# Attention with a following prelu layer on one core: when a group's half sums are swapped and added, and when its turned tiles are made, on VectorE

## The chip, the cores and the metric

The kernel runs on one core of a Trainium2 chip. The metric is device microseconds of one execution; the kernel before takes 435.62 us (median of 3 runs, 435.51 to 436.47).

## The reference, cut to what matters

```
q, k, v: (8 batches, 12 heads, 448 rows, 64)   g_q, g_k: (64,)
q_n = q / sqrt(mean(q*q, -1) + 1e-6) * g_q          # k_n likewise, with g_k
attn = softmax(q_n @ k_n^T / 8);   x = attn @ v      # heads side by side: (3584, 768)
h = x @ w_in                                         # (3584, 2048)
g = max(h, 0) + alpha * min(h, 0)
out = g @ w_out                                      # (3584, 768)
```

## The kernel before, in words

**Groups.** The 96 pairs of batch and head are taken four at a time: 24 groups `y`, three to a batch. The 448 rows of a head are 64 x 7, so a group has seven tiles of scores (y, 0) to (y, 6).

**Preparing a group** takes a chain over four engines. SyncE's queue loads q and k (`load_qk`). GpSimd squares them (L193). VectorE sums the squares: `reduce` (L214), one for q and one for k. From group 9 on the data lies so that a reduce gives half sums only: each partition has the sum over one half of the 64 columns. `fold` swaps the halves between blocks of 32 partitions (four short reductions, L231) and adds them (L234). ScalarE takes the root (`root`, L244 and L245, an Ln and an Exp), GpSimd scales q and k by it (`scale`, L251), VectorE transposes blocks of 32 x 32 (`flip`, L359, once for q and once for k), and ScalarE multiplies the turned k by the product of the two gains (`weigh`, L369). `turn` (L371) makes those flips of a group that are still missing.

**Bursts.** The instruction order is written out by a planner in bursts 0 to 68, each engine running its own list in order. In a burst TensorE makes two to four tiles of scores (L415) in the PSUM tiles `sc`, of which there are two, and ScalarE makes their exponentials (`soft`, L429). In some bursts TensorE also adds up the denominators (`dn` or `dnb`, L440 and L464, with ScalarE's `log` and `invert` behind them) and the product with v (`av`, `avb`, L440), which VectorE divides into `xT` (`muls`, L539).

**Units** fill the rest of a burst (`gaps[n]`, by a table at L998). `up(b, ft)` is one of 16 blocks of x @ w_in: six matmuls (L554), then alpha times it on ScalarE (L594), then the max on VectorE (L598), which frees the PSUM tile. `down` is one tile of g @ w_out; `quad_a`, `quad_b` and `quad_c` together make two tiles by the seven products of Strassen's scheme (L681), and VectorE adds each product up (L700, L705, L710, L722, L727, L729, L739, L744). Its operand sums are made by `mix_two` (L669, L670) and `mix_rest` (L677).

**PSUM tiles.** `hT`, `qx`, `qz`, `qc` and `dnb` take turns in two tiles; a name with an `a` behind it (`hTa`, `qza`, `qca`), `dn` and `av` share one more, "the wide one". A matmul into a tile waits until its last reader is through.

**Jobs.** What VectorE does to prepare groups is put behind units as jobs (`jobs[n]`). A `quad` takes one job behind a product and all that are left behind its last one, as here:

```
def quad_b(tile, spare, jobs=()):        # L715
    ...
    nc.vector.tensor_add(out=w, in0=p[:, :OH], in1=u2)            # L722
    some(jobs)                                                    # one job
    ...
    nc.vector.tensor_add(out=o, in0=z[:, :OH], in1=w)             # L727
    send(tile + 1, 1, o)
    nc.vector.tensor_add(out=u2, in0=z[:, :OH], in1=u2)           # L729
    while jobs:
        some(jobs)                                                # the rest
```

`quad_a` takes one job behind L700, one behind L705 and the rest behind L710; `quad_c` one behind L739 and the rest behind L744; a `down` takes all at its end, sums ahead of its copy (L627) and flips behind it. Behind an `up`, one job is taken, and from burst 20 on only after the first, third and fifth of a burst; what is left is done at the burst's end. The root of group y stands in burst `root_at[y]`, the reduces of most groups one burst earlier.

Of the kernel before, what the change touches and what calls it, by code (L numbers as in the profile page):

```python
# [21 lines left out]
def kernel(  # L22
# [27 lines left out]
    TD = min(3 * G, NG)  # L50
# [320 lines left out]
    def turn(y):  # L371

        if y >= TD:
            for nm in "qk":
                if (y, nm) not in qkT:
                    flip(y, nm)
            return
        if y <= G or y > 2 * G:
            ps = [psf.tile([128, 512], FP32, name="tps", tag="mm") for _ in "qk"]
        else:  # L380
            ps2 = psa.tile([128, 2, 512], FP32, name="tps2", tag="acc")
            ps = [ps2[:, 0], ps2[:, 1]]
        tps = [
            t[:, : S].bitcast(FP16).rearrange("p (j c) -> p j c", j=J) for t in ps
        ]
        for tp, nm in zip(tps, "qk"):
            for j in range(J):
                nc.tensor.transpose(
                    tp[:, j, :], qs[y, nm][:, j].rearrange("p h d -> p (h d)"), ident
                )  # L390
        for tp, nm in zip(tps, "qk"):
            t = att.tile([128, J, 2, 64], FP16, name=f"{nm}T", tag=f"{nm}T", bufs=2)
            o = t.rearrange("p j g c -> p j (g c)")
            if nm == "q":
                nc.vector.tensor_copy(out=o, in_=tp)
            else:
                nc.vector.tensor_scalar(
                    out=o, in0=tp, scalar1=gain[:, 0:1], scalar2=None, op0=ALU.mult
                )
            qkT[y, nm] = t  # L400
# [4 lines left out]
    def pre(ys):  # L405
        return len(ys) == 1 and ys[0] >= PRE and ys[0] % G == G - 1
# [205 lines left out]
    def down(tile, oh, jobs=(), spare=False):  # L612

        op = bank("op", spare)
        for ft in range(NF):
            nc.tensor.matmul(  # L616
                out=op[:, :OH],
                lhsT=gT[:, ft, ts(tile % J, 128)],
                rhs=w_out_sb[:, ft, ts(oh, OH)],
                start=(ft == 0),  # L620
                stop=(ft == NF - 1),
            )
        for f, a in jobs:
            if f not in (turn, flip, weigh):
                f(*a)
        o = result()
        nc.vector.tensor_copy(out=o, in_=op[:, :OH])  # L627
        for f, a in jobs:
            if f in (turn, flip, weigh):
                f(*a)  # L630
        send(tile, oh, o)
# [203 lines left out]
    while m < NG * J or steps:  # L835
        n = len(bursts)
# [20 lines left out]
        while len(bursts[n]) < limit and m < NG * J:  # L857
            y, j = divmod(m, J)
# [13 lines left out]
    def at(n, f, *a):  # L872
        prep.setdefault(max(int(n), 0), []).append((f, a))

    def after(n, f, *a):
        post.setdefault(max(int(n), 0), []).append((f, a))
# [7 lines left out]
        (y, den_at[y - 2] - pre((y - 2,))) for y in range(TD, NG) if y % G == 1  # L884
    )
    turns = {n: y for y, n in turn_at.items()}
    jobs, root_at, nexts = {}, {}, {}
    for y in range(G, NG):

        early = y < G + 2  # L890
        if early:
            n = turn_at[y - 1] + 1
        elif y == G + 2:
            n = den_at[G - 1]
        elif y == 2 * G:
            n = turn_at[y] - 4
        elif y % G == 1:
            n = den_at[y - 4] - 1 - pre((y - 2,))
        elif y % G:
            n = den_at[y - G] - pre((y - G,))  # L900
        else:
            n = av_at[y - 4]
        low = y > 3 * G + 1
        if low:
            nexts[root_at[y - 2]] = y
        elif y in (3 * G - 1, 3 * G):

            after(den_at[G] - (y < 3 * G), load_qk, y)
        else:
            at(n - (6 if early or y % G == G - 1 and pre((y - G,)) else 3 if y == 2 * G else 4 if y < 3 * G else 5), load_qk, y)  # L910
        root_at[y] = n + 1 + (y in (G + 2, 3 * G))
        third = y % G == G - 1 and pre((y - G,))
        for nm in "qk":
            if y != 2 * G:
                after(n - 2 - third + (low and y % G == 1) - (low and third and y != 20), square, y, nm)
            if early:
                after(n, reduce, y, nm, (0, 1) if (y, nm) == (G, "k") else None)
            else:
                now = jobs.setdefault(n + (y == G + 2 and nm == "k") - (low and third), [])
                now.append((reduce, (y, nm)))  # L920
                if nm == "k" and y > TD:
                    now.append((fold, (y,)))
        if y == 3 * G:
            after(n, *jobs[n].pop()[:1], y, "k")
        roots[root_at[y]] = y
    at(av_at[G] - 6, load_v, 1)
    for b in range(2, B):
        after(av_at[G * b - 1] + 1, load_v, b)
# [28 lines left out]
    gaps = [[] for _ in range(NB)]  # L957
# [148 lines left out]
    for n in range(NB):  # L1106
# [70 lines left out]
        if n in roots:  # L1177
            y = roots[n]
# [42 lines left out]
        ups_first = gaps[n] and gaps[n][0][0] is up  # L1221
# [7 lines left out]
        if flips:  # L1229
            jobs.setdefault(n, []).extend(flips)  # L1230
        turned = n in turns and gaps[n] 
        if turned and not ups_first and turns[n] >= TD:
            jobs.setdefault(n, []).extend([(turn, (turns[n],)), (weigh, (turns[n],))])
        elif turned and turns[n] >= TD:
            y = turns[n]
            todo = [(flip, (y, nm)) for nm in "qk" if (y, nm) not in qkT] + [(weigh, (y,))]
            jobs[n] = todo + jobs.get(n, [])
        elif turned and turns[n] != 2 * G + 1:
            turn(turns[n])
        for k, (f, a) in enumerate(gaps[n]):  # L1240
            if k == 1 and turned and turns[n] == 2 * G + 1:
                turn(turns[n])
            spare = k in spare_at or f is up and a in forced
            if f is down:
                down(*a, jobs.pop(n, ()), spare)
            elif f is not up:
                f(*a, jobs.pop(n, []))
            else:
                f(*a, spare)
                done += 1  # L1250
                if n in jobs and not (lead and done < 5) and (
                    n < av_at[2 * G - 1] or done % 2
                ):
                    g, c = jobs[n].pop(0)
                    g(*c)
                    if not jobs[n]:
                        del jobs[n]
                while late and done == late[0][0]:
                    _, g, c = late.pop(0)
                    g(*c)  # L1260
# [50 lines left out]
```

## Time and profile before

| | us |
|---|---|
| median of 3 runs | 435.62 |
| the profiled execution | 432.87 |
| its span, first to last instruction | 431.1 |
| TensorE busy (matmuls) | 404.6 |
| VectorE busy | 281.3 |
| ScalarE busy | 270.5 |
| GpSimd busy | 268.0 |

The profile is of one execution. Busy times are sums over an engine, so they do not tell which engine sets the time in which stretch. A row of the timeline has the start, the duration, the engine, the line, the operation, what it writes and reads, and how many were merged; in brackets stands how long the engine was idle just before and whose work ended that. The view of waits adds these up by pairs: total, times, longest. The view of windows gives, for a stretch, each engine's busy time and the clock granted to TensorE.

### The profile page before, as it was taken

What the parts mean: (1) busy time and instruction counts of PE and PEld (TensorE: products, weight loads), DVE (VectorE), ACT (ScalarE), POOL (GpSimd) and SP (SyncE); (2) the same over time, 40 slices, a digit from 0 to 9 for tenths busy, and PEclk for the clock granted to TensorE, in tenths of its full rate; (3) what the DMA queues carried; (4) which work ended last, traced back from release to release, by engine and by line L of the source; (5) the groups of instructions that cost most, each with busy time, mean ns of one, the idle gap of its engine ahead of it and who ended that gap; (6) DMA issues with size and microseconds to landing.
All of it is one profiled execution on the core that took longest, in us unless ns stands there. A gap on an engine that the chain in (4) does not pass through costs nothing.

```text
span 431.1 us, 11989 instructions
## 1 busy us (share of the span) xinstructions
PE 404.6 (94%) x5083; PEld 210.0 (49%) x5083; DVE 281.3 (65%) x495; ACT 270.5 (63%) x405; POOL 268.0 (62%) x184
## 2 busy tenths in 40 slices
PE   7789999999998989999999979899998999999996
PEld 3344454544545435544455435445454445655564
DVE  3876874576458576886879673977667745465322
ACT  5887777656845876467777785586576786125210
POOL 5699993698667969196571839367840715600780
PEclk9999999999999999999999998999999999999999
DMA  8899999957381996349581795449602600320133
GB/s 266 227 210 208 173 193 235 250 153 141 90 205 40 246 183 156 85 100 234 119 202 40 185 232 124 96 102 231 136 21 58 100 2 22 75 56 0 26 95 101
DMA packets 37221, 58.39 MB, mean 135 GB/s; under 512 B 4768, under 2 KB 28976, under 8 KB 37168
## 3 DMA queue, kind: packets, MB, share of 16 engines
q1 hardware_dynamic: 23232, 45.43, 41.8%
q0 software_dynamic: 13536, 11.81, 18.3%
q8 instruction: 39, 0.64, 0.6%
q10 hardware_dynamic: 400, 0.39, 0.3%
q14 instruction: 14, 0.11, 0.1%
HBM read 58.40 MB, written 11.01 MB: 161 GB/s over the span
## 4 chain that ended last, share of the span: by engine, by line
PE 53%; DVE 15%; DMA 11%; ACT 8%; POOL 7%; issue 3%; SPq 1%; DVEq 0%; POOLq 0%
PE hT L554 16%; PE hTa L554 6%; PE qx L681 5%; PE sc L415 4%; ACT expT L429 4%; PE oq L681 3%; DVE sp L214 3%; DMA nat<-in_k_dram 3%; DMA nat<-in_q_dram 3%; PE op L616 2%; PE qc L681 2%; DVE gT L598 2%; DMA arena<-in_k_dram 2%; PE qz L681 2%; PE oqm L681 2%
## 5 line engine op out<-in xcount | busy, mean ns | idle before, releaser
L429 ACT ACTIVATE expT<-sc 128x896 f16<-128x896 f32 x168 | 147.4, 912 | 43.9 <-PE sc L415 43.7
L554 PE MATMUL hT<-xT,w_in_sb 128*128 128x448 f16 x558 | 116.7, 353 | 4.5 <-DVE gT L598 4.0
L554 PEld LDWEIGHTS <-w_in_sb 128*128 128x128 f16 x768 | 73.0, 98 | 79.6 <-issue 15.4
L251 POOL TENSOR_TENSOR qs<-nat,rr 128x896 f16<-128x896 f32 x30 | 63.9, 2230 | 36.4 <-ACT rr L245 27.2
L594 ACT ACTIVATE gT<-hT,cols 128x448 f16<-128x448 f32 x92 | 58.1, 633 | 42.0 <-PE hT L554 42.0
L598 DVE TENSOR_TENSOR gT<-hT,gT 128x448 f16<-128x448 f32 x93 | 57.6, 620 | 39.9 <-ACT gT L594 39.6
L193 POOL TENSOR_TENSOR nat<-nat 128x896 f32<-128x896 f32 x30 | 50.6, 1691 | 37.9 <-DMA nat<-in_k_dram 22.1
L415 PE MATMUL sc<-qT,kT 64*32 64x448 f16 (+1 forms) x1092 | 53.8, 358 | 7.1 <-ACT expT L429 4.2
L681 PEld LDWEIGHTS <-gT 128*128 128x128 f16 x352 | 33.5, 98 | 25.1 <-issue 4.1
L554 PE MATMUL hTa<-xT,w_in_sb 128*128 128x448 f16 x198 | 42.8, 352 | 0.0
L539 DVE TENSOR_TENSOR xT<-av,rden 64x448 f16<-64x448 f32 (+1 forms) x37 | 27.2, 735 | 17.1 <-ACT expT L429 5.9
L415 PEld LDWEIGHTS <-kT 64*32 64x32 f16 (+1 forms) x1092 | 15.8, 93 | 40.5 <-issue 35.3
L214 DVE TENSOR_REDUCE sp<-nat 128x28 f32<-128x896 f32 x30 | 31.9, 1076 | 0.0
L594 ACT ACTIVATE gT<-hTa,cols 128x448 f16<-128x448 f32 x33 | 21.0, 636 | 16.3 <-PE hTa L554 16.3
L598 DVE TENSOR_TENSOR gT<-hTa,gT 128x448 f16<-128x448 f32 x33 | 20.4, 617 | 15.3 <-ACT gT L594 15.3
L616 PE MATMUL op<-w_out_sb,gT 128*128 128x384 f16 x160 | 27.4, 326 | 0.0
L440 PEld LDWEIGHTS <-vt 64*32 64x32 f16 x1344 | 19.8, 92 | 14.7 <-issue 5.4
L440 PE MATMUL av<-expT,vt 64*32 64x448 f16 x896 | 24.3, 350 | 2.4 <-DVE osb L729 1.3
L669 POOL TENSOR_TENSOR gs<-gT 128x1024 f16<-128x1024 f16 x3 | 6.4, 2123 | 30.4 <-DVE gT L598 28.1
L616 PEld LDWEIGHTS <-gT 128*128 128x128 f16 x192 | 18.0, 98 | 13.4 <-issue 2.2
L677 POOL TENSOR_TENSOR gT<-gT 128x1024 f16<-128x1024 f16 x11 | 23.8, 2166 | 0.0
L369 ACT ACTIVATE kT<-kT,gain 128x896 f16<-128x896 f16 x15 | 15.5, 1035 | 11.6 <-DVE kT L359 11.6
(152 smaller groups left out, 555.7 us busy)
## 6 DMA issues: line engine op xcount, KB each, us to landing
nat<-in_q_dram SPq DMA_DIRECT2D x60, 216.0 KB, 4.8
nat<-in_k_dram SPq DMA_DIRECT2D x60, 216.0 KB, 6.4
out_dram<-osb SPq DMA_DIRECT2D x107, 96.0 KB, 2.2
vt<-in_v_dram POOLq DMA_DIRECT2D x8, 672.0 KB, 12.3
w_in_sb<-in_moe_w_in_dram POOLq DMA_DIRECT2D x24, 128.0 KB, 5.2
w_out_sb<-in_moe_w_out_dram POOLq DMA_DIRECT2D x4, 768.0 KB, 10.7
nat<-in_k_dram SPq DMA_DIRECT2D x6, 448.0 KB, 5.6
nat<-in_q_dram SPq DMA_DIRECT2D x5, 448.0 KB, 5.7
```

The costliest lines, as they stand in the source:

```text
L193: nc.gpsimd.tensor_mul(out=sqs[y, nm], in0=t[:, :, :HD], in1=t[:, :, :HD])
L214: nc.vector.tensor_reduce(out=parts[y][:, ts("qk".index(nm), 4 * J), :1], in_=sqs[y, nm], axis=AXIS_X, op=ALU.add,)
L251: nc.gpsimd.tensor_mul(out=t.rearrange("p j d n -> p n j d"), in0=nat[y, nm][:, :, :HD].rearrange("p (n j) d -> p n j d", j=J), in1=r.unsq ...
L415: nc.tensor.matmul(out=sc[ds(64 * g + m * c, m), par, :S].rearrange("p (j c) -> p j c", j=J), lhsT=kT[ds(64 * par, 64), j, g, ts(c, m)], r ...
L429: nc.scalar.activation(out=expT[y][:, j], in_=scs[y, j][:, :, :S], func=AF.Exp, scale=QK_SCALE, bias=EXP_BIAS,)
L440: nc.tensor.matmul(out=accs[g][ds(32 * n, 32), :S], lhsT=weights(g, y, par, c, j), rhs=expT[y][ds(64 * g, 64), j, par, :], start=(j == 0), ...
L539: nc.vector.tensor_mul(out=x, in0=av, in1=r)
L554: nc.tensor.matmul(out=hT[:, :S], lhsT=w_in_sb[:, block_of(g, i), ts(ft, 128)], rhs=xT[b][:, g, i, :], start=(i == 0 and g == 0), stop=(i ...
L594: nc.scalar.activation(out=g, in_=hT[:, :S], func=AF.Copy, scale=alpha_sb[:, ft : ft + 1])
L598: nc.vector.tensor_max(out=g, in0=hT[:, :S], in1=g)
L616: nc.tensor.matmul(out=op[:, :OH], lhsT=gT[:, ft, ts(tile % J, 128)], rhs=w_out_sb[:, ft, ts(oh, OH)], start=(ft == 0), stop=(ft == NF - 1),)
L681: nc.tensor.matmul(out=bank[:, c], lhsT=g[:, ft], rhs=v[:, ft, c], start=(first and ft == 0), stop=(ft == HF - 1), skip_group_check=True,)
```

## The change

Three edits in the planner. The fold of a group is put one burst later if the root leaves room for it; the flips and the weigh of a group are single jobs, ahead of the others, in every burst whose units are not led by an `up`, where before `turn` was one job for both flips and stood last with the weigh; and behind the `up`s a job is also taken when no more units are left than jobs.

```
-    jobs, root_at, nexts = {}, {}, {}
+    jobs, root_at, nexts, folds = {}, {}, {}, []
...
                 now.append((reduce, (y, nm)))
                 if nm == "k" and y > TD:
-                    now.append((fold, (y,)))
+                    folds.append((n, y))
...
+    for n, y in folds:
+        jobs.setdefault(min(n + 1, root_at[y] - 1), []).append((fold, (y,)))
...
         turned = n in turns and gaps[n] 
-        if turned and not ups_first and turns[n] >= TD:
-            jobs.setdefault(n, []).extend([(turn, (turns[n],)), (weigh, (turns[n],))])
-        elif turned and turns[n] >= TD:
+        if turned and turns[n] >= TD:
             y = turns[n]
             todo = [(flip, (y, nm)) for nm in "qk" if (y, nm) not in qkT] + [(weigh, (y,))]
             jobs[n] = todo + jobs.get(n, [])
...
                 if n in jobs and not (lead and done < 5) and (
                     n < av_at[2 * G - 1] or done % 2
+                    or len(jobs[n]) >= (len(gaps[n]) - k - 1)
                 ):
```

In the built programs the lists of TensorE, ScalarE, GpSimd and SyncE are the same, instruction for instruction, and no instruction is added or dropped. VectorE's list is another order of the same instructions, in ten places (bursts in brackets; "max" is L598, sums and copies of products by their lines; Rq and Rk are the reduces, Fq and Fk the flips):

| place | before | after |
|---|---|---|
| A (23, 24) | max, Rq 10, max, max, Rk 10, max, fold 10, Fq 9 | max, Rq 10, max, Rk 10, max, fold 10, max, Fq 9 |
| B (26, 27) | Rq, Rk, fold 11, L627, L627 | Rq, Rk, L627, fold 11, L627 |
| C (31) | max, max, Rq 13, max, Rk 13, fold 13 | max, Rq 13, max, Rk 13, max, fold 13 |
| D (34, 35) | Rk 14, fold 14, L739, Fq 13, Fk 13, L744, L669 | Rk 14, L739, Fq 13, L744, Fk 13, fold 14, L669 |
| E (39) | max, max, Rq 16, max, max, Rk 16, fold 16 | max, Rq 16, max, Rk 16, max, fold 16, max |
| F (42, 43) | L710, fold 17, L722, Fq 16, Fk 16, L727, L729, L483 | L710, L722, Fq 16, L727, L729, Fk 16, fold 17, L483 |
| G (47) | max, max, Rq 19, max, Rk 19, fold 19 | max, Rq 19, max, Rk 19, max, fold 19 |
| H (50, 51) | Rk 20, fold 20, max, Fq 19, max, Fk 19, L483 | Rk 20, max, Fq 19, max, Fk 19, fold 20, L483 |
| I (55) | L700, Rq 22, L705, Rk 22, L710, fold 22, max | L700, L705, Rq 22, L710, Rk 22, fold 22, max |
| J (58, 59) | Rk 23, fold 23, L722, Fq 22, Fk 22, L727, L729, L483 | Rk 23, L722, Fq 22, L727, L729, Fk 22, fold 23, L483 |

## The prediction

> **What bounds the kernel now.** I read the page first.
>
> ```profile
> PE 404.6 (94%) x5083; PEld 210.0 (49%) x5083; DVE 281.3 (65%) x495; ACT 270.5 (63%) x405; POOL 268.0 (62%) x184
> ...
> PE 53%; DVE 15%; DMA 11%; ACT 8%; POOL 7%; issue 3%; SPq 1%; DVEq 0%; POOLq 0%
> ```
>
> TensorE is busy 94% of the span; the chain that ended last runs through VectorE (DVE) for 15%. Only VectorE's order changes, so a gain can come only out of TensorE's waits for VectorE, and a loss is a new one. The waits of TensorE:
>
> ```profile
> PE hT L554 <- DVE gT L598: 4.0, 10, 1.7
> PE dn L440 <- DVE gT L598: 3.1, 1, 3.1
> ...
> PE av L440 <- DVE osb L729: 1.3, 2, 1.1
> ...
> PE av L440 <- DVE osb L744: 0.7, 1, 0.7
> ```
>
> Some 9 us in all. Whether one of them is worth its length is a local question: is what TensorE meets next also late? So I went through the timeline of all engines at each of the ten places, putting VectorE's new order on the old starts. Steps from start to start come from those rows: a reduce 1.0 to 1.1 us, a fold 1.1, a max 0.5, a flip or a product's sum 0.45 to 0.55. VectorE may read a product 0.2 us after TensorE starts its next one (at 316.25 and 316.45), a max starts 0.04 after ScalarE's row ends.
>
> **Place F** decides most:
>
> ```profile
> 227.65 0.85 DVE L231 TENSOR_REDUCE sp<-sp 32x56 f32<-32x56 f32 x4
> ...
> 228.72 0.55 DVE L722 TENSOR_TENSOR osb<-qz,osb 128x384 f32<-128x384 f32 x1
> 229.19 0.63 DVE L359 STREAM_TRANSPOSE qT<-qs 128x448 f32<-128x448 f32 x1
> 229.74 0.60 DVE L359 STREAM_TRANSPOSE kT<-qs 128x448 f32<-128x448 f32 x1
> ...
> 230.38 1.04 ACT L369 ACTIVATE kT<-kT,gain 128x896 f16<-128x896 f16 x1 [1.56 <-DVE kT L359]
> 230.71 0.54 DVE L729 TENSOR_TENSOR osb<-qza,osb 128x384 f32<-128x384 f32 x1
> 231.18 0.67 DVE L483 COPY rden<-dnb 128x224 f32<-128x224 f32 x2
> ...
> 231.33 1.70 ACT L429 ACTIVATE expT<-sc 128x896 f16<-128x896 f32 x2
> ...
> 238.12 0.54 PE L554 MATMUL hT<-xT,w_in_sb 128*128 128x448 f16 x2 [0.37 <-DVE xT L539]
> ```
>
> See that the fold at 227.65 ran while VectorE had nothing else: `qz` is readable only at 228.65 (`qza` starts at 228.45). See also that ScalarE's weigh waits for the k flip, and the exponentials, for which TensorE's next scores need room, queue behind it. New: L710 ends 227.62; L722 waits to 228.65; q flip 229.1; L727 waits to 230.05 (the scores start at 229.85); L729 230.5; k flip 230.95 to 231.55. The weigh starts at 231.6 instead of 230.38: **+1.2** for both pairs of exponentials, the scores and `qc`. The fold now stands in a stretch without idle time: the copies of `rden` start at 232.6 instead of 231.18, **+1.4**, and VectorE stays busy up to the second pair of L539 (236.81), for which the hT at 238.12 waits. F costs **1.4** (bounds: -0.2, if only the wait of `av` of 0.21 counted; 1.6, with its rounding).
>
> **J** has the same order but another start. L722 goes from 326.80 to 325.9 (`qza` starts at 325.69), L727 waits to 327.3 (scores at 327.08), L729 327.75, k flip 328.2 to 328.8; the weigh starts 328.85 against 328.46: +0.4. `rden` is 0.6 later, but VectorE idled 2.29 us ahead of L539 (332.22), which covers that. TensorE's wait of 1.06 ahead of `av` (329.38) goes, and the scores behind it then wait for the exponentials. **+0.4** (-1.06 to 0.6).
>
> **H.** Without the fold the max of up 14 still waits for ScalarE to 275.15, that of up 15 to 276.48 (its L594 ends 276.44); flip k 277.0, fold 277.55, `rden` 278.6 against 278.16. No idle time follows up to the second L539 (283.90 to 285.15), so xT is 0.45 late; the last two matmuls of the hT at 284.49 need it 0.76 in, at 285.25, so **+0.4**. Weigh, exponentials and `av` come 0.6 earlier: worth nothing while xT ends last (bounds -0.6 to 0.45).
>
> **E.** A reduce ahead of each max moves the max of up 10 from 208.31 to 209.36; up 12 needs its tile and starts at 210.0, not 208.97. Three ups of 1.13 later up 15 starts at 213.4, not 212.84 (where it waited for the max of up 12, which VectorE's saturated list gives at the same time). Scores and ScalarE's run from 214.17, on the chain, follow: **+0.5** (0 to 1.05).
>
> **I.** L705 goes ahead of the reduces (298.87), L710 300.33, Rk 300.8, fold 301.9; the max of up 10 ends 304.12 instead of 303.77 and `qz` (303.96) waits for its tile: **+0.2** (0 to 0.35).
>
> **D** looks like the gain: L744 ends at 180.9 instead of 182.46, so `av` need not wait 0.71. But VectorE has no gap from 178.17 to 188.75, and the same work ends at the same time: L700 stays at 187.55, and the product at 188.15, which waited 0.30 for it, waits about 0.9. **0** (-0.7 to 0.1).
>
> **C, G**: up 12 (155.65) and up 11 (252.00) start 1.0 later, for the reason of E, but at 160.88 and 259.15 TensorE waits 1.67 and 3.09 us for a max that VectorE's full list puts at the same time: the wait moves forward, **0** (up to 0.1 at G, where Rk needs a square that ends at 253.10). **A**: the up at 107.11 finds its tile free at 106.9: 0. **B**: the fold goes into the 1.28 us of idle time ahead of 129.25: 0. If A's and B's covers were gone they would cost 0.1 and 1.1.
>
> Sum: 1.4 + 0.4 + 0.4 + 0.5 + 0.2 = **+2.9 us**. Nothing downstream takes it up: from 238 to 251 and from 286 to 298 TensorE runs on without idle brackets, and from 331 on no such wait is over 0.27. No DMA or semaphore work is added; loads follow their scales, so they move along.
>
> **The clock.** At G there is a second effect:
>
> ```profile
> 255.71:259.12 3.41, 0.35 (x16) 0.08 (x1) 3.38 (x7) 2.64 (x5) 2.06 (x1) 1.00 1.16 229
> 259.12:262.53 3.41, 3.38 (x65) 1.42 (x65) 0.51 (x1) 0.11 (x1) 3.41 (x3) 0.50 0.12 20
> ```
>
> A row gives the stretch and its length, busy time and count of PE, PEld, DVE, ACT and POOL, and, third from the right, the clock granted to TensorE: after 3.41 us with 0.35 us of matmuls it was 0.50 for 3.41 us. From the `dn` there (259.15) to the next product took 3.12 us against 1.63 at 312.01 to 313.64, plus 0.1 in the product: the drop costs 1.6. With the wait split, TensorE is idle 2.1 us in one piece, busy 1.3 of 3.41. The windows of 3.41 us with 2.01 busy (from 16.77) and 2.35 (from 327.39) led to no drop. 1.3 lies between 0.35 and 2.01, so the trace does not decide. The Trainium skill (TensorE: Matmul & The Clock Gate, Part 1: The HAM clock gate) says that the gate looks at free-running windows of 3413 ns and halves the clock after an idle one; the rows agree on length and factor, and by that rule the drop comes in some executions only.
>
> On the profiled execution's 432.87 the sum gives 435.8 with the drop kept, 434.2 without. The runs' median is 2.75 above that execution. The three runs lie within 1.0 of each other, less than a drop costs, so they show no mixture of executions with and without it, and I take both kernels' runs to be alike in it: 435.62 + 2.9 = **438.5**.
>
> **Rivals.**
> - *The drop goes too* (18%): the timed executions had it and lose it: 2.9 - 1.6 = +1.3, 436.9. For it: the one profiled execution had it. Against: nothing shows that the timed ones did, and 1.3 us of matmuls may still be too few to keep the clock.
> - *The wide tile decides* (14%, faster): where L729, L744 and the max come earlier, `av` does, and if the scores behind it find `sc` free, that is kept: D 0.71, F 0.21, H 0.47, J 1.06 gained, 2.45, less E and I: -1.75, 433.9. It decides if the exponentials at these places are done before `av` ends. For it: those idle brackets name VectorE. Against: at 280.16, the row behind `av` at H, TensorE waits 0.91 more for ScalarE.
> - *Taken up* (10%): no delay outlasts its burst, because a wait further on already covers it, as at C and G: 435.6.
> - *Loads late too* (6%): F's late scale of group 17 (236.22) delays the load of group 19, whose k square (251.42) waited 3.25 us for its DMA; one more 1.2 at G: +4.1, 439.7.
> - *My sum* 52%.
>
> **Numbers.** Bounds of the terms alone: from about 1 to 4.1. From 434.6 to 439.8 the range leaves out the second rival and little else. A measurement can tell about 0.2% (0.87 us). Faster 0.14, same 0.10, slower 0.76.
>
> **What would show it.** F right: ScalarE's wait ahead of the weigh of group 16 grows from 1.56 to 2.8 and TensorE waits ahead of the scores. J and D: the waits of 1.06 and 0.71 ahead of `av` are gone, those behind them longer. E: up 12 waits 1.3 instead of 0.26. G: 1.0 ahead of up 11, 2.1 ahead of `dn`. Wrong: L722 or L727 starting before I let them, or `hT` at F less than 1 us later against `qx` of place F (222.63).

## The result and the profile after

| | before | after |
|---|---|---|
| median of the timed executions, us | 434.83 (20 runs, 433.10 to 436.92) | 437.73 (20 runs, 434.70 to 439.97) |
| ratio, 95% interval | | 1.0068 (1.0045 to 1.0091) |
| the profiled execution, its span | 432.87, 431.1 | 435.54, 433.7 |

The change makes the kernel slower by 0.68%, which is 2.9 us (2.0 to 4.0). The sum on record was +2.9. The ratio of only_folds, below, leaves out two disturbed executions of 443 and 444 us, which its median includes.

The head of the page of after, busy times by engine and then the chain that ended last:

```profile
PE 403.9 (93%) x5083; PEld 209.8 (48%) x5083; DVE 282.4 (65%) x495; ACT 270.6 (62%) x405; POOL 268.3 (62%) x184
...
PE 54%; DMA 11%; DVE 11%; POOL 10%; ACT 5%; issue 5%; SPq 2%; DVEq 0%; POOLq 0%
```

The counts are those of before, and the busy times agree within 1.1 us: no work came or went. VectorE's share of the chain even fell from 15% to 11% while the kernel became slower, so these shares do not show the loss. TensorE's waits do (engine, line, whose work ended the wait, then the sum, the number and the longest):

```profile
PE sc L415 <- ACT expT L429: 6.1, 10, 0.9
PE hT L554 <- DVE gT L598: 5.7, 9, 1.3
PE dn L440 <- DVE gT L598: 2.4, 1, 2.4
...
PE qx L681 <- DVE osb L700: 1.1, 1, 1.1
```

The waits ahead of `av` that named L729 and L744, 2.0 us in all, are gone. In their place the scores wait 6.1 us in ten places for ScalarE instead of 4.2 in seven, the product at place D waits 1.05 instead of 0.30, and the ups wait 1.7 more for a max.

Sums over the whole span do not tell what was kept. Since every engine but VectorE runs the same list in both kernels, I set the same instruction of both traces side by side and took the difference of their starts, and from its steps what each place adds:

| place | what it adds, us | put at | what the rows show |
|---|---|---|---|
| A, B | 0 | 0 | |
| C | 0.0 | 0 | up 12 waits 1.26 instead of 0.27, the next wait is 0.68 instead of 1.67 |
| D | +0.1 | 0 | weigh and exponentials 0.6 earlier, given back at L700 |
| E | +0.54 | 0.5 | up 12 waits 1.25 instead of 0.26; kept |
| F | +1.47 | 1.4 | kept from the second pair of L539 on |
| G | +0.27 | up to 0.1 | and, besides, no drop of the clock there: -1.59 |
| H | +0.45 | 0.4 | weigh 0.6 earlier, worth nothing; xT late |
| I | +0.07 | 0.2 | |
| J | +0.34 | 0.4 | |
| sum of the order | **+3.3** | **+2.9** | |

To reach the +2.6 between the two spans one adds two things that are not the order's: full clock at G (-1.59), and the +0.92 by which after is behind before it reaches place C. The profiled execution of after has half the clock from 12.79 to 16.21 us, where that of before has full clock; but that of only_turns, below, is 0.92 behind there as well, with full clock throughout, so how much of the 0.92 is the clock's stays open.

The steps of E, H and J come out the same wherever the same order was run again (the runs are described below): E adds 0.53 or 0.54 in all four kernels that have its new order, H 0.45 in four, J 0.34 in two. Place E after is this row; before, the wait in its bracket was 0.26:

```profile
211.01 1.29 PE L554 MATMUL hT<-xT,w_in_sb 128*128 128x448 f16 x6 [1.25 <-DVE gT L598]
```

**Place F after**, from the timeline of all engines:

```profile
230.23 0.56 DVE L722 TENSOR_TENSOR osb<-qz,osb 128x384 f32<-128x384 f32 x1 [1.03 <-PE qz L681]
230.71 0.63 DVE L359 STREAM_TRANSPOSE qT<-qs 128x448 f32<-128x448 f32 x1
231.53 0.56 DVE L727 TENSOR_TENSOR osb<-qza,osb 128x384 f32<-128x384 f32 x1 [0.19 <-PE qza L681]
...
232.47 0.64 DVE L359 STREAM_TRANSPOSE kT<-qs 128x448 f32<-128x448 f32 x1
233.14 0.85 DVE L231 TENSOR_REDUCE sp<-sp 32x56 f32<-32x56 f32 x4
233.14 1.04 ACT L369 ACTIVATE kT<-kT,gain 128x896 f16<-128x896 f16 x1 [2.75 <-DVE kT L359]
...
234.21 0.68 DVE L483 COPY rden<-dnb 128x224 f32<-128x224 f32 x2
...
235.04 0.38 PE L415 MATMUL sc<-qT,kT 64*32 64x448 f16 x8 [0.91 <-ACT expT L429]
...
241.17 0.54 PE L554 MATMUL hT<-xT,w_in_sb 128*128 128x448 f16 x2 [0.37 <-DVE xT L539]
```

L722 idles 1.03 us where the fold stood before, and L727 0.19. ScalarE waits 2.75 ahead of the weigh (before 1.56; 2.8 was expected), so the exponentials and TensorE's next scores are late. The fold now runs between the k flip and the copies of `rden`. These start 3.03 later than before, and the hT at 241.17 starts 3.05 later, of which 1.58 had come before the place: 1.47 is F's.

**Place G**, the windows of 3.41 us (length; busy time and count of PE, PEld, DVE, ACT, POOL; granted clock; DMA share; GB/s):

```profile
258.55:261.96 3.41, 1.55 (x22) 0.56 (x21) 3.34 (x8) 3.31 (x7) 1.58 (x1) 1.00 1.16 229
261.96:265.37 3.41, 2.90 (x72) 1.71 (x72) 0.99 (x2) 1.11 (x2) 3.41 (x3) 1.00 0.17 29
```

With TensorE's wait cut into 1.26 ahead of up 11 and 2.37 ahead of `dn`, the window holds 1.55 us of matmuls, and the next one has full clock. Before, with a wait of 3.09 in one piece, 0.35 us of matmuls in a window were followed by half the clock.

### The profile page after: what moved, and what is told of

Same layout as the page of the kernel before. It is cut to its first block, busy times and chain, and to the rows that moved or that the text cites. A ratio compares the mean times of both kernels' runs of the same rounds, so it can differ in the third digit from the quotient of the medians.

```text
span 433.7 us, 11994 instructions
## 1 busy us (share of the span) xinstructions
PE 403.9 (93%) x5083; PEld 209.8 (48%) x5083; DVE 282.4 (65%) x495; ACT 270.6 (62%) x405; POOL 268.3 (62%) x184
## 4 chain that ended last, share of the span: by engine, by line
PE 54%; DMA 11%; DVE 11%; POOL 10%; ACT 5%; issue 5%; SPq 2%; DVEq 0%; POOLq 0%
PE hT L554 15%; DMA nat<-in_k_dram 7%; PE hTa L554 5%; PE qx L681 5%; PE sc L415 5%; PE op L616 4%; PE oq L681 3%; POOL qs L251 2%; ACT expT L429 2%; DMA arena<-in_k_dram 2%; PE qz L681 2%; DVE gT L598 2%; PE av L440 2%; PE qc L681 2%; ACT gT L594 2%
## 5 line engine op out<-in xcount | busy, mean ns | idle before, releaser
L598 DVE TENSOR_TENSOR gT<-hT,gT 128x448 f16<-128x448 f32 x93 | 57.7, 621 | 40.1 <-ACT gT L594 40.0
L193 POOL TENSOR_TENSOR nat<-nat 128x896 f32<-128x896 f32 x30 | 50.8, 1698 | 39.3 <-DMA nat<-in_k_dram 24.3
L539 DVE TENSOR_TENSOR xT<-av,rden 64x448 f16<-64x448 f32 (+1 forms) x37 | 27.2, 735 | 16.6 <-ACT expT L429 5.8
L214 DVE TENSOR_REDUCE sp<-nat 128x28 f32<-128x896 f32 x30 | 32.0, 1076 | 0.7 <-POOL nat L193 0.7
L598 DVE TENSOR_TENSOR gT<-hTa,gT 128x448 f16<-128x448 f32 x33 | 20.5, 621 | 15.9 <-ACT gT L594 15.9
L669 POOL TENSOR_TENSOR gs<-gT 128x1024 f16<-128x1024 f16 x3 | 6.4, 2122 | 30.4 <-DVE gT L598 28.1
```

Source lines behind the costliest of these rows:

```text
L193: nc.gpsimd.tensor_mul(out=sqs[y, nm], in0=t[:, :, :HD], in1=t[:, :, :HD])
L214: nc.vector.tensor_reduce(out=parts[y][:, ts("qk".index(nm), 4 * J), :1], in_=sqs[y, nm], axis=AXIS_X, op=ALU.add,)
L539: nc.vector.tensor_mul(out=x, in0=av, in1=r)
L598: nc.vector.tensor_max(out=g, in0=hT[:, :S], in1=g)
```

## Experiments

Two theories stand at the start. The one on record: the order costs about 2.9, nearly half of it at F. The rival: most of what the order costs is covered by waits further on, and the timed difference comes from the clock or from something not seen. Totals below are ratios of timed executions; what a place does is read from one profile each, by the differences of starts as above. All totals are against the kernel before, run on the same chip.

**only_often: the third edit alone**, a job also where no more units are left than jobs; it changes the order at C, E, G and A.

```
                     n < av_at[2 * G - 1] or done % 2
+                    or len(jobs[n]) >= (len(gaps[n]) - k - 1)
```

> The third edit alone: jobs behind more of the ups, which moves places A, C, E and G and nothing else. Theory (a late max holds back the next up wherever VectorE's list has room later): E +0.5 us, G +0.3 ahead of dn, A and C nothing, so +0.8 for the order; the wait ahead of dn is split (about 1.3 and 2.4 instead of 0.27 and 3.09), and with it the drop of the clock at 259 us does not come. Rival (the change costs time only through the clock, not through the order): ScalarE's rows behind E stand where they stood, and the kernel is not slower.

Measured: 433.15 against 435.15 us, ratio 0.997 (0.9925 to 1.0015). E adds 0.53, as the order's theory has it. At G the `dn` waits 2.09 and comes no later for the new order (0.01 the other way), and no drop follows: -1.6 net. At I, which this edit does not touch, this execution loses 1.52:

```profile
296.61 1.68 POOL L193 TENSOR_TENSOR nat<-nat 128x896 f32<-128x896 f32 x1 [2.33 <-DMA nat<-in_k_dram]
296.62 2.21 DVE L670 TENSOR_TENSOR arena<-arena,gT 128x1024 f16<-128x1024 f16 x1
...
298.76 0.55 DVE L700 COPY osb<-qx 128x384 f32<-128x384 f32 x1
...
299.36 1.46 PE L681 MATMUL qx<-arena 128*128 128x384 f16 x8 [1.49 <-DVE osb L700]
```

The same rows before:

```profile
297.45 0.69 DVE L670 TENSOR_TENSOR arena<-arena,gT 128x1024 f16<-128x1024 f16 x1
...
297.70 1.98 POOL L193 TENSOR_TENSOR nat<-nat 128x896 f32<-128x896 f32 x1 [2.32 <-DMA nat<-in_k_dram]
```

L670 took 2.21 us instead of 0.69 when GpSimd's square began 0.01 us before it, and GpSimd's square took 1.98 instead of 1.68 when L670 had begun first. Which comes first hangs on when the load of k lands. What follows: the order's theory holds for E; in this execution the clock at G gave back more than E cost; and a profile can be 1.5 us longer at a place that no edit touches, so a total says nothing of a single place.

**only_turns: the second edit alone**, the flips and the weigh as single jobs ahead of the others.

```
-        if turned and not ups_first and turns[n] >= TD:
-            jobs.setdefault(n, []).extend([(turn, (turns[n],)), (weigh, (turns[n],))])
-        elif turned and turns[n] >= TD:
+        if turned and turns[n] >= TD:
```

> The second edit alone: flips as single jobs, places D, F, I and J; every fold stays where it was. Theory (the k flip, and the weigh behind it on ScalarE, decide): F +1.2 at ScalarE's weigh and at the next up, J +0.9 (k flip behind L727, which waits for TensorE to 327.3, and L729), D +0.45 at its weigh but nothing at L700, I nothing: +2.1. Rival (the fold's new place is what costs): no more than 0.3.

Measured: 435.79 against 435.15, ratio 1.0024 (1.0 to 1.0048). At F the weigh comes 1.19 later, as expected, but the up behind it only 0.44: here the fold still stands ahead of L722, so the copies of `rden` are not held back. D returns to 0, J adds 0.93. The order comes to +1.4, where 2.1 had been expected; the miss is F's route through ScalarE, which costs 0.44 and not 1.2. This execution also has a drop of two windows at G, behind a window with 1.33 us of matmuls (the rows below), and at I, where L670 took 2.08 us, it loses 1.4:

```profile
256.09:259.50 3.41, 1.33 (x21) 0.43 (x20) 3.31 (x9) 2.93 (x7) 1.10 (x1) 1.00 1.13 236
259.50:262.91 3.41, 2.41 (x56) 1.29 (x63) 1.48 (x3) 0.26 (x1) 3.41 (x3) 0.50 0.49 83
262.91:266.33 3.42, 3.42 (x32) 1.35 (x10) 0.00 (x0) 2.54 (x3) 3.42 (x2) 0.50 0.16 43
```

**only_folds: the first edit alone**, the folds a burst later.

```
-                    now.append((fold, (y,)))
+                    folds.append((n, y))
...
+    for n, y in folds:
+        jobs.setdefault(min(n + 1, root_at[y] - 1), []).append((fold, (y,)))
```

> The first edit alone: folds one burst later, places B, D, F, H and J, while both flips stay one job, which now comes behind the fold and, at F and J, behind L729. Theory: F +1.9 at the weigh (k flip ends 232.25), J +1.1, H +0.4, B and D nothing at L700: +3.4, more than the whole change. Rival (the fold costs its own length where no idle time covers it, and the flips do not matter): F +1.0, H +0.4, J nothing: +1.4.

Measured: 440.03 against 435.15, ratio 1.0085 (1.0052 to 1.0117), the costliest of the three. F's weigh is 2.07 late, since the fold runs ahead of the flips there, and the up behind it 1.32; J adds 1.22, H 0.45, D 0. The order comes to +3.0, near the 3.4 expected and far from the rival's 1.4. The later fold is what costs; the single flips alone cost less.

**after_pairs: the change with both flips as one job ahead of the fold**, where the burst is not led by an `up`. This puts the weigh back where it was and leaves the fold late.

```
-        if turned and turns[n] >= TD:
+        if turned and not ups_first and turns[n] >= TD:
+            jobs[n] = [(turn, (turns[n],)), (weigh, (turns[n],))] + jobs.get(n, [])
+        elif turned and turns[n] >= TD:
```

> The changed kernel with both flips of a group as one job again where a quad or a down leads, ahead of the fold: at F and J the k flip stands ahead of L727, the fold behind L729. Theory: at F ScalarE's weigh is back at its old place (-0.1), but the fold still makes rden and xT 1.0 late, so F +1.0; at J the weigh comes 0.9 earlier than in the kernel before and rden's 0.2 is covered, so J -0.8; E +0.5, G +0.3, H +0.4, I nothing: +1.4 against before, 1.5 less than the change. Rival (only the k flip matters at F): F 0, and +0.4 against before.

Measured: 437.08 against 435.15, ratio 1.0043 (1.0015 to 1.007). Place F in its timeline:

```profile
231.32 1.04 ACT L369 ACTIVATE kT<-kT,gain 128x896 f16<-128x896 f16 x1 [1.51 <-DVE kT L359]
...
232.22 0.85 DVE L231 TENSOR_REDUCE sp<-sp 32x56 f32<-32x56 f32 x4
...
233.30 0.68 DVE L483 COPY rden<-dnb 128x224 f32<-128x224 f32 x2
```

ScalarE waits 1.51 as before the change, the weigh is not late at all (-0.06), and still the up behind the place is 1.14 late: the fold of 1.1 us ahead of `rden` makes 1.14 of F's 1.47 without any late weigh, and the other 0.33 comes with the single flips. At J, on the other hand, the weigh comes 0.9 earlier and 0.7 of it is kept. At D the weigh is 1.24 earlier and nothing of it is kept (0.04). At I, where nothing was expected, this edit moves something too: both reduces come behind L710, the product `qz` then waits 0.98 for a max, and 1.03 is lost, besides 1.36 at L670, which took 2.05 us. With the 1.03 the order comes to +2.5, where 1.4 had been expected.

**after_f_back: the change with place F put back** as it was before.

```
     for n, y in folds:
-        jobs.setdefault(min(n + 1, root_at[y] - 1), []).append((fold, (y,)))
+        n = n - 1 if y == 17 else min(n + 1, root_at[y] - 1)
+        jobs.setdefault(n, []).append((fold, (y,)))
...
+            if turned and turns[n] == 16:
+                jobs[n] = [(turn, (16,)), (weigh, (16,))]
```

> The changed kernel with place F alone put back (fold 17 ahead of L722, both flips of group 16 ahead of L727). Theory (the order at F costs 1.47 us of the change): ScalarE's rows between E and G stand as in the kernel before plus E's 0.5, everything else as in the changed kernel, so 1.5 us less than the change. Rival (F's delay would have been swallowed by the next late place, G, whose wait is 2.4 us long): the up behind F is 1.5 earlier, but dn at G is not, and the kernel is as slow as the changed one.

Measured: 436.44 against 434.43, ratio 1.0046 (1.0014 to 1.0079). F adds 0.00 in its profile, so its 1.47 comes from the order there. G adds 0.62 instead of 0.27. That is no part of F's delay that G would take up: the reduce of k waits there for a square whose load landed 0.34 late in this execution (more on this below, at G). The total is +2.0 (0.6 to 3.4), which is 0.9 below the change's +2.9, with intervals that overlap, so the totals alone do not tell what F is worth.

**mix_early12 and mix_early14: the kernel before, with the operand sums of two products on GpSimd some bursts earlier.** These two are not parts of the change. They ask whether TensorE's waits, which the change only moves, go when VectorE's full list at G and at I is relieved of the 1.4 us of `mix_two` (L669, L670). The first moves those of product 12 to burst 44, the second those of product 14 to burst 52.

```
+    early = {12: 44}                       # the second: {14: 52}
     for n, y in ((33, 6), (36, 8), (41, 10), (48, 12), (55, 14), (57, 16), (62, 18)):
-        at(n, mix_two, y, nc.vector)
+        at(early.get(y, n), mix_two, y, nc.gpsimd if y in early else nc.vector)
         at(n, mix_rest, y)
```

> The kernel before with one thing moved: the two sums for tile 12 (L669, L670), which stand in VectorE's full list ahead of dn at G, are made by GpSimd four bursts earlier, in a stretch where it waits 9.2 us for ScalarE's root. Theory (a wait of 3.09 us in one piece is what halves the clock): the wait ahead of dn shrinks by the two sums, 1.33 us, to about 1.75, the clock is not halved there, and the next rows come 1.33 + 1.5 = 2.8 us earlier than in the profile before; fewer executions have half-clock stretches. Rival (the drop does not hang on this wait): -1.3 and the drop stays.

Measured: 431.32 against 434.43, ratio 0.9926 (0.9894 to 0.9959). The wait ahead of `dn` is 1.76 instead of 3.09, no drop follows, and G gives 2.92 (2.8 expected): 1.33 by the shorter wait and 1.59 by the clock. The emptiest window there, counted in steps of 3.413 us from this execution's drop at 20.63, holds 1.66 us of matmuls:

```profile
256.15:259.56 3.41, 1.66 (x51) 0.77 (x57) 3.16 (x8) 2.85 (x6) 3.41 (x2) 1.00 1.15 233
```

This execution loses 1.45 of it at I again, where L670 took 2.15.

> The kernel before with the two sums for tile 14 (L669, L670, ahead of L700 at place I) made by GpSimd three bursts earlier. Two of the profiles so far show L670 at 2.1 to 2.2 us instead of 0.69 there, where GpSimd's square of the same moment had started first. Theory (a VectorE sum of two 16-bit operands cannot run beside a GpSimd instruction, and the stall delays all of VectorE's list): with no such sum there, nothing at 295 to 301 us can stall; ScalarE's first max behind I stands 0 to 0.2 earlier than in the profile before in every execution, and 1.3 to 1.5 earlier than in executions with the stall. Rival (the stall comes from the late DMA of the k half of group 22): the reduce of k waits for its square and ScalarE's row is as late as with the stall.

Measured: 433.89 against 434.43, ratio 0.9976 (0.995 to 1.0003), which is no difference that can be told. The profile shows I 0.13 earlier and no stall there, and the drop at G unchanged, behind a window with 1.11 us of matmuls.

**best: the kernel before, with those two moves, the same for product 8 (burst 36), and the folds 14 and 23 later**, at D and J, behind both flips:

```
-    jobs, root_at, nexts = {}, {}, {}
+    jobs, root_at, nexts, folds = {}, {}, {}, {}
...
-                    now.append((fold, (y,)))
+                    if y in (14, 23):
+                        folds[n] = y
+                    else:
+                        now.append((fold, (y,)))
...
+    early = {8: 36, 12: 44, 14: 52}
...
             jobs.setdefault(n, []).extend([(turn, (turns[n],)), (weigh, (turns[n],))])
+            if n in folds:
+                jobs[n].append((fold, (folds[n],)))
```

> A version from what the runs show, from the kernel before: the sums for tiles 8, 12 and 14 on GpSimd, early; at D and J the fold one burst later, behind both flips as one job (D: L739, both flips, L744, fold; J: L722, both flips, L727, L729, fold); F, H, E and I in the old order. Theory: D -1.0 (VectorE has 1.37 us less ahead of L700, and av starts 0.7 earlier), G -1.33 and no drop of the clock there (-1.5 where there was one), I 0 to -1.5, J -0.7: -3.0 by order alone against the profile before, -4.5 with the drop, ratio about 0.99. Rival (GpSimd's earlier sums run into its own work or slow VectorE's): D and G give back what they gain, and the kernel is within 0.5 us of the one before.

Measured: 429.55 against 434.43, ratio 0.9895 (0.9858 to 0.9932): 4.6 us faster than before by the ratio (3.0 to 6.2), and below the changed kernel. Its waits and, from its timeline, place D:

```profile
PE dn L440 <- DVE gT L598: 1.8, 1, 1.8
```

```profile
186.72 0.55 DVE L700 COPY osb<-qx 128x384 f32<-128x384 f32 x1
...
187.32 1.46 PE L681 MATMUL qx<-arena 128*128 128x384 f16 x8
```

D gives 1.44 (1.0 expected), G 2.92, I 0.13, J 0.7 to 0.9. At D a later fold, which the change has too, pays once the 1.4 us of sums no longer stand in VectorE's list between L744 and L700: after_pairs has the same order there with the sums left in, and keeps 0.04. (Sums moved without the fold were not run at D.)

**Steps and totals together.** In eight of the nine kernels the steps of the order alone add up to a number inside the interval of the total; the ninth is mix_early12 (-1.3 by order, -2.9 with the clock at G, -4.6 to -1.8 by the total), where it takes the clock.

## Why the prediction came out right, and where its terms were off

**The method.** The view of waits shows 9 us for VectorE. What carried the prediction is that it asked at each place whether the next thing on TensorE's path is late too, and put the new order on the old starts. Eight of ten places came out within some 0.1 us. At F the sign named for it, `hT` at least 1 us later against `qx`, is there with 1.47.

**F, 1.4 put, 1.47 measured.** The amount and the mechanism of the larger term were right: the fold, out of a gap, stands ahead of `rden`, and nothing up to the second L539 makes it good. The +1.2 through the weigh and the exponentials stood beside it as a second route of nearly the same length. It is not one: with that route alone the up is 0.44 late (only_turns), with the fold alone 1.14 (after_pairs).

**E, H, J, and C, A, B**: as put. J's bound of -1.06 was nearer than it looked: with pairs of flips the same place gains 0.7.

**D, 0 put, +0.1.** Right for the reason given: `av` is earlier, VectorE's list is full up to L700, and the product there waits 1.05 (put at 0.9):

```profile
189.19 1.46 PE L681 MATMUL qx<-arena 128*128 128x384 f16 x8 [1.05 <-DVE osb L700]
```

best shows the other half of it: take 1.4 us out of that full list and D gains 1.44.

**G, up to 0.1 put, 0.27 measured.** Here the size of the term was wrong, by the prediction's own rows. In the new order a max starts at 252.32 and Rk could follow at 252.85, but "a square that ends at 253.10" holds it until then. The max behind it then starts at 254.1 and the fold at 254.76 instead of 254.50: 0.26, and not 0.1 at most. In the profile of after it is just this: the square is 3.03 later than before where everything around it is 3.05 later, and Rk waits for it (the first row is from before, the others from after):

```profile
251.42 1.68 POOL L193 TENSOR_TENSOR nat<-nat 128x896 f32<-128x896 f32 x1 [3.25 <-DMA nat<-in_k_dram]
...
254.45 1.68 POOL L193 TENSOR_TENSOR nat<-nat 128x896 f32<-128x896 f32 x1 [3.44 <-DMA nat<-in_k_dram]
...
256.16 1.09 DVE L214 TENSOR_REDUCE sp<-nat 128x28 f32<-128x896 f32 x1 [0.18 <-POOL nat L193]
```

The term moves with the landing of that load: set against the delay around it, the square comes 0.29 earlier in only_often, 0.19 earlier in after_pairs and 0.34 later in after_f_back, and the place costs 0.0, 0.09 and 0.62. So a load can shift a place by 0.3 either way from one execution to the next. "Nothing downstream takes it up" stands: F's delay is still there at the end of after.

**I, 0.2 put, 0.07 at most.** The max of up 10 was expected to hold `qz`; its tile came free at the moment the product was due.

**The clock.** "I take both kernels' runs to be alike in it" cannot be read from one profile, nor from three runs within 1.0 of each other: the 20 executions of before lie 3.8 apart. In the ten profiles the drop at G goes with the wait ahead of `dn`. It is there in all four that have the 3.09 us in one piece (before, only_turns, only_folds, mix_early14) and in none of the six with a split or shorter wait, and where it is missing the rows behind come 1.59 earlier, which is the 1.6 of the prediction.

Other executions have no trace, but each lists its mean granted clock. A window of 3.41 us at half the clock takes 1.7 us off clock times span, so (1 - clock) x span / 1.7 is the number of such windows (up to half a one of it lies in the last 2 us of the span, behind most of the work). Averaged over the executions of a kernel that is 1.8 and 2.0 for before on the two chips, 1.6 for after, 1.0 for only_often, 1.7 for only_turns, 2.6 for only_folds, 1.7 for after_pairs, 1.6 for after_f_back, 0.9 for mix_early12, 1.8 for mix_early14 and 1.1 for best. Among 150 executions of eleven series, compared within each series, a window more goes with 1.05 us more (standard error, the uncertainty of the figure itself: 0.1).

That after gets something back by the clock is therefore not shown. It has 0.2 to 0.4 of a window less than before has on two other chips (no clock is on record for the 20 executions of before next to it), with a standard error of 0.3. If it were so, 3.3 less 0.2 to 0.4 would be 2.9 to 3.1; the 3.3 too lies within the measured interval. "The drop goes too" happened in the profile of after but not in the total: its +1.3 lies outside 2.0 to 4.0. For only_often, which has the orders of A, C, E and G alone, nearly one window less (standard error 0.4), some 0.9, is of the size to make up for E; this is argued from averages and not shown. That prediction and result agree to a tenth is partly chance: the order read from the profiles is some 0.4 dearer than put, and the total is known to 1.0 only.

**The other rivals.** "The wide tile decides" is refuted: `av` comes earlier, and the scores behind it wait, at J for 0.91 and 0.42:

```profile
332.94 0.38 PE L415 MATMUL sc<-qT,kT 64*32 64x448 f16 x8 [0.91 <-ACT expT L429]
333.75 0.38 PE L415 MATMUL sc<-qT,kT 64*32 64x448 f16 x8 [0.42 <-ACT expT L429]
```

"Loads late too" did not occur: the square at G came 3.03 later where all else was 3.05 later. "Taken up" holds at C and D, as the sum had it, and at none of E, F, H and J, whose delays last to the end.

What stays open: executions of one kernel lie up to 5 us apart (after). The number of windows at half clock explains 42% of their variance in the fit above. The stall of L670 at I, about 1.4 us in four of the eight profiles that have it on VectorE there, is of the size to make much of the rest, but only a profile shows it, so that this is its cause is argued and not shown.

## What to carry to other kernels

Before moving a step into another slot of an engine whose list is in order, lay the new order on the old starts and look at the first thing that is late behind it: a wait that goes is worth nothing if the same engine is full up to the next release, and a step that sat in a gap becomes dear once it stands in a full stretch. To shorten a wait for a full engine, take work off that engine (here two sums of 0.7 us, given to GpSimd some bursts earlier) rather than reorder it. A change of one microsecond has to be read place by place in the profiles, and its total taken over many executions: the third edit costs 0.5 at its place and nothing that the total can tell.

## What the runs showed of the hardware that was not expected

**The clock falls behind a window that is not idle.** From 80 us up to the end of TensorE's work, half the clock appears four times in the ten profiles, always within or behind place G. In the window of 3.41 us ahead TensorE was busy for 0.35 (before), 1.11 (mix_early14), 1.17 (only_folds) and 1.33 us (only_turns), so up to 39%. In each profile the stretches of half clock begin whole numbers of 3.413 us apart (in only_folds at 11.69, 264.28 and 438.36 us), so the windows can be counted on from one to the next; at G 1.55 us (45%, after) and 1.66 us (49%, mix_early12) led to no drop. The limit for these stretches lies between. In the first 25 us drops also followed windows with 0.87 to 2.01 us (25% to 59%), while a window with 2.01 us led to none in before, so the busy share as the profile counts it is not the whole rule. The Trainium skill (TensorE: Matmul & The Clock Gate, Part 1: The HAM clock gate) has the clock halved after an idle window of 3413 ns; the lengths agree with the rows (3.41), the word idle does not, and the measurement decides. That page also says that the window runs free of the kernel's start; the rows agree: counted back in steps of 3.413 us from the first drop, at 12.79 us in after and at 20.63 in mix_early12, a window begins 2.55 and 0.15 us behind the kernel's start.

**VectorE's 16-bit sums and GpSimd hold each other up.** L669 and L670 take 0.64 to 0.69 us alone. Beside a GpSimd instruction that began first and had 1.5 us or more still to run they took 1.91 to 2.40 (2.40 at 164.81 in before; 2.05 to 2.21 at I in four profiles), each ending only after GpSimd's had; with less left to run they took less (1.23 with 0.88 left, at 163.54 in before). Where L670 began first at I, GpSimd's L193 took 1.93 to 2.23 instead of 1.68. Flips (0.60 to 0.70), sums with a PSUM operand (0.51 to 0.56) and reduces (1.05 to 1.09 for L214) take as long beside GpSimd as without it. The Trainium skill (SBUF — State Buffer, Who interferes with whom) says that a VectorE instruction with two SBUF inputs contends with a GpSimd instruction that reads SBUF, and that the two share one port pair, which one holds for its whole instruction; these rows agree with it.
